# A training step of one transformer block: the backward loop's first four units of exponentials made in the stage ahead of it

## The chip, the cores and the metric

The kernel runs on one core of one Trainium2 chip. The core has five engines with a queue of instructions each: TensorE (PE), VectorE (DVE), ScalarE (ACT), GpSimd (POOL) and SyncE (SP, which here only issues DMAs). Each queue is worked off in order; engines wait for one another through semaphores. The metric is the device time of one execution in microseconds. Before the change it is 2457.15 us, the median of three runs (2454.79 to 2458.89).

## The reference

One block (2048 tokens, width 512, 32 heads of 16, an MLP of 1792 with squared ReLU, modulation from a condition vector c) is run forward, and its vector-Jacobian product is taken for all inputs and weights. Cut to what matters:

```python
h = layernorm(x) * (1 + ca) + sa
qkv = h @ wqkv                                   # 32 heads of 16
p = softmax(q @ k^T / 4)
x = x + ga * ((p @ v) @ wo)
h = layernorm(x) * (1 + cb) + sb
x = x + gb * (relu(h @ w1 + b1) ** 2 @ w2 + b2)
# outputs: x, and the gradients of A_x, wqkv, wo, w1, b1, w2, b2, c, w_mod for a given grad_out
```

## The kernel before, in words

The kernel has four parts that matter here.

*The forward attention loop.* For each of 4 chunks of 512 queries, 8 groups of 4 heads and 16 tiles of 128 keys it makes one unit: scores on PE, exponentials on ACT into a tile ET (128 x 4 x 512, bf16, four buffers), and the product with the values on PE. The MLP, forward and backward, of the chunks already done is woven in between, unit by unit.

*The last stage* (`last_chunk`, line 1265). When the forward loop is over, the MLP of the last chunk of 512 tokens stands alone, from about 1000 to 1101 us. Its order is written out by hand. `dh` (line 1417) makes the gradient at the MLP's input with w1T, a turned copy of w1 that is loaded in seven pieces. `mlp` (line 1469) makes the MLP's output, one token tile of 128 at a time, with 14 matmuls into one PSUM tile; its hooks name work that is put behind the matmul of that number. `grad` (line 1464) makes dO, the gradient of the attention's output, of one token tile. Weight gradients are "chains" (`add_chain`, line 227): four matmuls into a PSUM tile `pc` (three buffers), which DVE adds to a partial sum fetched from DRAM (line 238), and a DMA that stores the result. The four last chains, for out_3, put their results into `iqs` (two), `dpad` and `dwlast`, which SP stores. `later` puts off a DMA by a number of ticks, so the order of SP's queue is that of the ticks. SP's and ACT's DMAs share eight semaphores in turn: a DMA also waits until the one that last used its semaphore has landed. In this stage SP loads the tiles of the first head group, the token-major K (`KS_tok`) and dO of all tokens (`dOs_tok`, lines 1507 to 1509: three quarters from DRAM, the last, line 1518, from SBUF), turns the last chunk's dO by transposing DMAs and stores it.

*The backward attention loop* (line 1784 on). 8 head groups x 4 chunks of keys x 16 tiles of queries = 512 units, in 128 blocks of 4. A unit needs: scores s (4 matmuls, line 1634, in the PSUM banks A, B and C), exponentials e (4 of 128 x 512 on ACT, line 1640, into a tile E_u of four buffers), D (twice: 2 matmuls for dP into psD_u, line 1654, then DVE multiplies it with E_u into dS_u, line 1656), q (k products from dS_u, line 1715, then v products from E_u and dOs_tok, line 1724), a transpose of dS_u by SP's DMA or by PE (t, T), and for each block the dQ products (d, Q). The order within a block is a string of such tokens, one for even and one for odd blocks. D and q run behind the scores: at the start of block b the next D is number 8b - 1 and the next q number 8b - 4, where a number below zero does nothing. f is a keep-warm matmul (`keep_warm`, line 1680) that reads KS_tok and dOs_tok and adds nothing that counts. All queues of the loop, PE's, ACT's, DVE's, SP's and POOL's, follow the order of these strings. POOL clears the tiles of head group 1 at the front of the loop (`head_fill`, line 1785).

*The end*: the gradient at the block's input and of wqkv.

SBUF is given out in pools from two sides. A tile that is put where others lay waits for the last reader and writer of each of them.

## Time and profile before

One execution was profiled: 2456.11 us, with a span of 2454.3 us in the profile and a mean granted clock of 0.989. The median of the three timed runs is 2457.15 us.

| stretch (us) | PE busy | DVE busy | ACT busy | POOL busy | clock |
|---|---|---|---|---|---|
| 1060 to 1080, last stage | 20.00 | 16.84 | 6.36 | 0.00 | 1.00 |
| 1080 to 1100, last stage | 17.88 | 13.73 | 2.10 | 0.00 | 1.00 |
| 1100 to 1120, front of the loop | 17.71 | 14.17 | 13.90 | 8.85 | 0.74 |
| 1120 to 1140 | 19.43 | 18.54 | 18.72 | 0.00 | 1.00 |
| 1160 to 1180 | 19.39 | 19.22 | 19.87 | 1.99 | 1.00 |

Times within the profile are in us from the start of the span. A line of a timeline has the start, the duration, the engine (a q behind its name is its queue, with waits and DMA issues), the line of the kernel, the operation, what it writes <- what it reads, a count where equal instructions are merged, and in brackets how long the engine had stood idle and what ended that. The granted clock is that of TensorE as a share of its full speed.

### The profile page before, as it was taken

The numbers are of one execution on the slowest core, as the hardware profiler recorded it, in microseconds if no ns is written. First come the engines' busy times: TensorE is split into PE (matmuls) and PEld (weight loads), VectorE is DVE, ScalarE is ACT, GpSimd is POOL, SyncE is SP. The second block draws the span as 40 slices with busy tenths as digits, with TensorE's granted clock in tenths as the row PEclk, the third lists the DMA queues.
The fourth block names the chain that finished last, engine by engine and source line by source line (L and its number), as shares of the span: only waits on it lengthen the run. The fifth ranks groups of instructions, "written<-read, shape, count | busy, mean of one in ns | idle before, by whom it ended". The sixth has DMA issues, their size and how long they took to land.

```text
span 2454.3 us, 49932 instructions
## 1 busy us (share of the span) xinstructions
PE 2309.1 (94%) x18994; PEld 775.8 (32%) x18994; DVE 1843.5 (75%) x2390; ACT 2297.7 (94%) x3560; POOL 494.3 (20%) x664
## 2 busy tenths in 40 slices
PE   8899899989998999899999999999999999999999
PEld 3232233223322332442333233323233322323344
DVE  6555464355445554668999999999999989999975
ACT  8999999999998999639999999999999999999964
POOL 3111222332544353300111101101011010110100
PEclk9999999999998999999999999999999989999999
DMA  4578554266647874989999999999999999999995
GB/s 149 135 167 195 177 147 99 85 169 135 96 93 152 153 139 90 237 242 186 209 199 210 205 209 205 203 207 208 204 208 200 204 199 198 208 199 219 200 260 181
DMA packets 1192303, 440.58 MB, mean 180 GB/s; under 512 B 1068283, under 2 KB 1161913, under 8 KB 1191550
## 3 DMA queue, kind: packets, MB, share of 16 engines
q1 hardware_dynamic: 1155214, 392.23, 81.3%
q0 software_dynamic: 19872, 27.09, 7.1%
q10 hardware_dynamic: 16976, 18.07, 2.7%
q8 instruction: 149, 2.44, 0.4%
q14 instruction: 92, 0.75, 0.1%
HBM read 98.83 MB, written 72.63 MB: 70 GB/s over the span
## 4 chain that ended last, share of the span: by engine, by line
ACT 39%; PE 36%; issue 10%; DVE 7%; DMA 5%; POOL 1%; DVEq 0%; SPq 0%; ACTq 0%; POOLq 0%
ACT E_u L1640 24%; ACT ET L580 13%; PE dqacc L1742 5%; PE psST L578 3%; PE psS_A L1634 3%; DMA dsT<-dS_u 3%; PE accVK L1715 2%; PE psS_B L1634 2%; PE psS_C L1634 2%; PE pm L234 2%; PE oacc L594 2%; PE pm L502 2%; PE pdh L1935 2%; PE pm L412 2%; PE pwq L1968 2%
## 5 line engine op out<-in xcount | busy, mean ns | idle before, releaser
L1656 DVE TENSOR_TENSOR dS_u<-psD_u,E_u 128x1024 bf16<-128x1024 f32 x1024 | 1185.4, 1218 | 59.9 <-PE psD_u L1654 19.6
L580 ACT ACTIVATE ET<-psST 128x1024 bf16<-128x1024 f32 x1024 | 941.6, 1268 | 12.6 <-PE psST L578 12.1
L1640 ACT ACTIVATE E_u<-psS_A 128x512 bf16<-128x512 f32 x768 | 496.8, 647 | 8.3 <-PE psS_C L1634 5.9
L1640 ACT ACTIVATE E_u<-psS_B 128x512 bf16<-128x512 f32 x768 | 490.3, 638 | 6.1 <-PE psD_u L1654 1.9
L1654 PE MATMUL psD_u<-iv,ido 32*128 32x512 bf16 x2048 | 408.6, 386 | 0.9 <-DVE dS_u L1656 0.9
L578 PE MATMUL psST<-qt_sb,kt_sb 32*128 32x512 bf16 x2048 | 312.5, 386 | 38.5 <-ACT ET L580 34.8
L1640 ACT ACTIVATE E_u<-psS_C 128x512 bf16<-128x512 f32 x512 | 329.8, 644 | 2.4 <-PE psS_B L1634 0.9
L1634 PE MATMUL psS_A<-ik,iq 32*128 32x512 bf16 x768 | 292.5, 381 | 14.1 <-ACT E_u L1640 1.7
L1634 PE MATMUL psS_B<-ik,iq 32*128 32x512 bf16 x768 | 293.6, 382 | 8.4 <-ACT E_u L1640 1.0
L1763 POOL TENSOR_TENSOR dQacc<-dQacc,dqtmp 128x512 f32<-128x512 f32 x64 | 81.2, 1268 | 838.3 <-ACT dqtmp L1758 838.3
L1634 PEld LDWEIGHTS <-iq 32*128 32x128 bf16 x2048 | 130.4, 91 | 325.3 <-issue 310.4
L1715 PE MATMUL accVK<-dS_u,qz 128*32 128x512 bf16 x2048 | 212.6, 389 | 0.2 <-DVE dS_u L1656 0.2
L594 PE MATMUL oacc<-ET,vaug 128*32 128x512 bf16 x2048 | 207.2, 395 | 3.9 <-DVE ostage L598 3.9
L1724 PE MATMUL accVK<-E_u,dOs_tok 128*16 128x512 bf16 x2048 | 202.5, 384 | 0.0
L1634 PE MATMUL psS_C<-ik,iq 32*128 32x512 bf16 x512 | 194.1, 379 | 4.0
L578 PEld LDWEIGHTS <-kt_sb 32*128 32x128 bf16 x2048 | 84.9, 91 | 316.8 <-issue 298.3
L1742 PE MATMUL dqacc<-dsT,KS_tok 128*32 128x512 bf16 x2048 | 146.7, 384 | 14.8 <-ACT E_u L1640 1.1
L252 DVE COPY part<-pm 128x512 f32<-128x512 f32 (+2 forms) x106 | 65.2, 615 | 120.9 <-PE pm L234 115.2
L1654 PEld LDWEIGHTS <-ido 32*128 32x128 bf16 x2048 | 105.4, 91 | 93.2 <-issue 81.2
L1827 ACT ACTIVATE dsT<-ptT 128x1024 bf16<-128x1024 bf16 x126 | 132.8, 1054 | 1.4 <-PE ptT L1688 1.3
L1715 PEld LDWEIGHTS <-qz 128*32 128x32 bf16 x2048 | 58.3, 94 | 177.1 <-issue 162.2
L1763 POOL TENSOR_TENSOR dQst<-dQacc,dqtmp 128x512 bf16<-128x512 f32 x31 | 39.3, 1267 | 265.1 <-ACT dqtmp L1758 265.1
(423 smaller groups left out, 2672.7 us busy)
## 6 DMA issues: line engine op xcount, KB each, us to landing
p_st<-part POOLq DMA_DIRECT2D x36, 256.0 KB, 4.8
kt_sb<-qkT_st POOLq DMA_DIRECT2D x124, 64.0 KB, 3.3
wA<-in_B_w_dram SPq DMA_DIRECT2D x28, 256.0 KB
wB<-w1T_st SPq DMA_DIRECT2D x21, 256.0 KB
wA<-w2T_st SPq DMA_DIRECT2D x21, 256.0 KB
wB<-in_B_w_dram SPq DMA_DIRECT2D x21, 256.0 KB
p_st<-part POOLq DMA_DIRECT2D x28, 192.0 KB, 4.7
p_st<-part SPq DMA_DIRECT2D x18, 256.0 KB
```

The lines of the kernel that those rows point to most:

```text
L578: PE.matmul(ps[:, hi, :], kt_sb[r:r + 32, kt * P:(kt + 1) * P], qt_sb[r:r + 32, :], start=True, stop=True, tile_position=(r, 0))
L580: ACT.activation(ET[:, 2 * pair:2 * pair + 2, :], ps[:], AF.Exp, scale=SCALE)
L594: PE.matmul(oacc[32 * hq:32 * hq + 32, :], lhsT, ET[:, hq, :], start=(kt == 0), stop=(kt == TT - 1), tile_position=(0, 32 * hq), skip_grou ...
L1634: PE.matmul(psS[:], st["q"][r:r + 32, qt * P:(qt + 1) * P], st["k"][r:r + 32, kc * 512:kc * 512 + 512], start=True, stop=True, tile_positi ...
L1640: ACT.activation(bst[u][0][:, hq, :], sst.pop((u, hq))[:], AF.Exp, scale=SCALE)
L1654: PE.matmul(psD[:, hi, :], st["do"][r:r + 32, qt * P:(qt + 1) * P], st["v"][r:r + 32, kc * 512:kc * 512 + 512], start=True, stop=True, til ...
L1656: DVE.tensor_tensor(dS_u[:, 2 * pair:2 * pair + 2, :], psD[:], E_u[:, 2 * pair:2 * pair + 2, :], ALU.mult)
L1715: PE.matmul(cur["vk"][32 * hq:32 * hq + 32, :], hst[hg]["qz"][:, qt, hq, :], bst[u][1][:, hq, :], start=(qt == 0), stop=False, tile_positi ...
L1724: PE.matmul(acc[32 * hq:32 * hq + DH, :], dOs_tok[:, qt, (hg * 4 + hq) * DH:(hg * 4 + hq + 1) * DH], E_u[:, hq, :], start=False, stop=(qt ...
L1742: PE.matmul(acc[32 * hq:32 * hq + 32, :], KS_tok[:, kc * 4 + kt, h * DH:h * DH + 32], tT[:, :, hq * 4 + kt, :], start=(kt == 0), stop=(kt ...
L1763: POOL.tensor_tensor(dst2, dst, tmp[:], ALU.add)
L1827: ACT.activation(dst, pt[:], AF.Identity)
```

## The change

The exponentials of units 0 to 3, which block 0 of the backward loop made, are now made in the last stage, each unit behind a hook of `mlp` or between two chains. Their tiles come from one pool of four buffers, opened ahead of both loops, that also serves ET, E_u, and w1T in four tiles of up to four pieces' width. dOs_tok no longer has a place during the stage: the last chunk's dO goes to DRAM (`dOs_st`), and all four quarters are loaded by POOL's queue at the front of the loop, into a tile laid out once the stage's pool `dwr` (dpad, xlast, dwlast) is released. Block 0 gets its own string of tokens, without scores and exponentials, with pairs of filler matmuls (i) at its front and keep-warm matmuls among its D and q.

```diff
+    epool = tc.alloc_tile_pool(name="phE", bufs=4, reuse_waits="tile")
+    def exp_tile(name):
+        return epool.tile([P, 4, 512], BF, name=name, tag="E")
...
-            ET = ework.tile([P, 4, 512], BF, name="ET", tag="ET")
+            ET = exp_tile("ET")
...
-                    PE.matmul(pdh[:], dzT[:, fc, ti * P:(ti + 1) * P], w1T[:, fc, :],
+                    PE.matmul(pdh[:], dzT[:, fc, ti * P:(ti + 1) * P], w1T[fc // 4][:, fc % 4, :],
...
+            def first_exps(u, tags):
+                keep["E", u] = E = exp_tile("E_u")
+                acc = [pools["mm"].tile([P, 512], F32, name="psSe", tag=t, bufs=3 if t == "pc" else 4) for t in tags]
+                for hq in range(4):
+                    r = 32 * hq
+                    PE.matmul(acc[hq][:], hsets[0]["q"][r:r + 32, u * P:(u + 1) * P], hsets[0]["k"][r:r + 32, 0:512],
+                              start=True, stop=True, tile_position=(r, 0))
+                for hq in range(4):
+                    ACT.activation(E[:, hq, :], acc[hq][:], AF.Exp, scale=SCALE)
...
-            keep["dOs"] = dpool.tile([P, TT, D], BF, name="dOs_tok", tag="dt")
-            for i in range(QC - 1):
-                later(2 + 2 * i, sp, keep["dOs"][:, 4 * i:4 * i + 4, :], dOs_st[:, 4 * i:4 * i + 4, :])
             mlp(0, {5: lambda: finish_dx(3), 7: lambda: turn_da(2), 11: lambda: grad(1)})
             sp(dx1_st[:, ts, :], dx1_c)
-            mlp(1, {3: lambda: turn_da(3), 7: lambda: grad(2)})
-            mlp(2, {3: lambda: grad(3)})
+            mlp(1, {3: lambda: turn_da(3), 7: lambda: grad(2), 12: lambda: first_exps(0, ("pc", "pc", "pc", "pm"))})
+            mlp(2, {3: lambda: grad(3), 9: lambda: first_exps(1, ("pc", "pc", "pm", "pm"))})
...
-            later(1, sp, keep["dOs"][:, ts, :], dOs_c[:])
+            later(1, sp, dOs_st[:, ts, :], dOs_c[:])
             store_grad(c, 1, dOT, dlt, 1)
-            mlp(3, {5: head_do})
+            mlp(3, {5: head_do, 10: lambda: first_exps(2, ("pc", "pc", "pm", "pm"))})
...
-            fill(3)
+            fill(2)
+            first_exps(3, ("pm",) * 4)
+            fill(1)
             flush_sums(True)
...
-                dpool = tc.alloc_tile_pool(name="dpool", bufs=1, reuse_waits="tile", side="right")
                 dwr = tc.alloc_tile_pool(name="dwr", bufs=1, reuse_waits="tile", side="right")
-                w1T = dpool.tile([P, FC, D], BF, name="w1T_1", tag="dt")
+                w1T = [exp_tile("w1T_1") for _ in range(4)]
...
-                    sp(w1T[:, 2 * s:2 * s + 2, :], w1T_st[:, 2 * s:2 * s + 2, :])
+                    sp(w1T[s // 2][:, 2 * (s % 2):2 * (s % 2) + 2, :], w1T_st[:, 2 * s:2 * s + 2, :])
...
         dwr.release()
-    KS_tok, dOs_tok = keep["KS"], keep["dOs"]
+    dpool = tc.alloc_tile_pool(name="dpool", bufs=1, reuse_waits="tile", side="right")
+    KS_tok, dOs_tok = keep["KS"], dpool.tile([P, TT, D], BF, name="dOs_tok", tag="dt")
...
-                bst[u] = [ework.tile([P, 4, 512], BF, name="E_u", tag="E_u"), None]
+                bst[u] = [exp_tile("E_u"), None]
...
+        order_0 = (
+            "i D i D i D q q q q q f f D q D f f D q f f D f q D f f ").split(), ""
         load_head(0)
+        for u in range(4):
+            bst[u] = [keep["E", u], None]
...
+            for i in range(QC):
+                POOL.dma_start(out=dOs_tok[:, 4 * i:4 * i + 4, :], in_=dOs_st[:, 4 * i:4 * i + 4, :])
             head_fill(1)
...
-                toks, bank = order_t if on_pe(b - 1) else order_n
+                toks, bank = order_0 if b == 0 else order_t if on_pe(b - 1) else order_n
...
-                        if b < 2 and i % 2 == 1:
-                            if nq > 0:
-                                keep_warm()
-                            elif nq < 0:
-                                PE.matmul(idle[:], ones_bf[:], identb.unsqueeze(1).to_broadcast([P, 4, P]), start=True, stop=True)
+                        if b == 1 and i % 2 == 1:
+                            keep_warm()
+                    elif c == "i":
+                        for _ in range(2):
+                            PE.matmul(idle[:], ones_bf[:], identb.unsqueeze(1).to_broadcast([P, 4, P]), start=True, stop=True)
```

More of the change, by code (lines that the diff above doesn't have):

```diff
@@ L1834 @@
         dq_last = hst[HG - 1]["dq"]
+    epool.release()
     with ExitStack() as ph:
```

## The prediction

> **What bounds the kernel now.** I read the page first, then the busy time by stretches of 20 us, the timeline of each engine between 1080 and 1130 us (the end of the dense stage and the front of the backward loop), the issues of DMAs, and the granted clock by stretches of 1 us.

> The page: busy share and instructions of each engine, and the chain that ended last.

> ```profile
> PE 2309.1 (94%) x18994; PEld 775.8 (32%) x18994; DVE 1843.5 (75%) x2390; ACT 2297.7 (94%) x3560; POOL 494.3 (20%) x664
> ACT 39%; PE 36%; issue 10%; DVE 7%; DMA 5%; POOL 1%; DVEq 0%; SPq 0%; ACTq 0%; POOLq 0%
> ```

> PE and ACT are both full on average, so an exponential moved out of the loop is worth something only where it is not replaced by another limit. The change touches about 50 us. By stretches (busy us of PE, PEld, DVE, ACT, POOL; granted clock; DMA share; GB/s):

> ```profile
> 1080.00:1100.00 20.00, 17.88 (x87) 7.48 (x85) 13.73 (x27) 2.10 (x8) 0.00 (x0) 1.00 0.90 241
> 1100.00:1120.00 20.00, 17.71 (x99) 4.00 (x98) 14.17 (x14) 13.90 (x26) 8.85 (x5) 0.74 0.92 216
> 1140.00:1160.00 20.00, 19.45 (x196) 6.02 (x188) 19.35 (x18) 19.96 (x40) 0.00 (x0) 1.00 1.19 221
> ```

> ACT has 18 us of 20 free before the loop, DVE loses about 5 us in the loop's first 20, and from 1140 PE, DVE and ACT are all at 97% or more. Timeline at the border:

> ```profile
> 1086.13 0.41 DVE L238 TENSOR_TENSOR dwbuf<-pc,dwbuf 128x256 bf16<-128x256 f32 x1
> 1090.06 0.38 PE L267 MATMUL rsums<-gfprod,ones_bf 128*1 128x512 bf16 x1 [1.50 <-DVE gfprod L1479]
> 1100.27 0.68 DVE L238 TENSOR_TENSOR dwlast<-pc,part 128x512 bf16<-128x512 f32 x1
> 1101.00 0.37 PE L1634 MATMUL psS_A<-ik,iq 32*128 32x512 bf16 x1 [0.86 <-DVE dwlast L238]
> 1110.10 0.60 PE L1681 MATMUL accVK<-dOs_tok,KS_tok 128*16 128x512 bf16 x1
> 1112.99 0.60 PE L1634 MATMUL psS_C<-ik,iq 32*128 32x512 bf16 x1
> 1124.08 0.39 PE L1634 MATMUL psS_A<-ik,iq 32*128 32x512 bf16 x1
> ```

> The stage ends with DVE's dwlast at 1100.95. PE starts the loop's block 0 at 1101.00, block 1 at 1112.99, block 2 at 1124.08: 12.0 and 11.1 us, where a later block takes (2344.3 - 1124.5)/126 = 9.68 us (start of block 2's first exponential to the end of the last, 126 blocks). So 3.7 us is all that the ramp of these two blocks can give back. PE first reads dOs_tok at 1110.10. SP's queue in the same time:

> ```profile
> 1088.56 0.32 SPq L179 DMA_DIRECT2D dx_st<-dx_c  x1
> 1093.72 5.62 SPq L179 DMA_TRANSPOSE dOT<-dOs_c  x4
> 1107.84 0.40 SPq L179 DMA_DIRECT2D out_dram<-dwlast  x1
> ```

> and issues by POOL (KB each, median us to landing), with the clock by 1 us:

> ```profile
> p_st<-part POOLq DMA_DIRECT2D x36, 256.0 KB, 4.8
> kt_sb<-qkT_st POOLq DMA_DIRECT2D x124, 64.0 KB, 3.3
> ```
> ```profile
> 1104.00:1105.00 1.00, 0.71 (x3) 0.28 (x3) 1.00 (x2) 0.57 (x2) 1.00 (x2) 0.87 0.99 352
> 1105.00:1106.00 1.00, 0.93 (x2) 0.10 (x1) 0.14 (x1) 0.82 (x3) 1.00 (x1) 0.50 0.50 143
> 1114.00:1115.00 1.00, 1.00 (x9) 0.10 (x1) 0.97 (x1) 0.72 (x2) 0.00 (x0) 0.51 1.29 215
> ```

> The clock was 0.50 from 1104.9 to 1115.0, though PE was busy for nearly all of it.

> **The change, part by part.**

> *Four batches of first exponentials in the stage.* 16 score matmuls and 16 exponentials of 128x512 move forward; the list of instructions of the changed program shows them there, and from block 1 on PE's and ACT's lists are as before. ACT has the room (2.10 us busy of 20). PE has not (17.88 of 20). The first batch stands behind the 13th matmul of the second tile's product, which PE reaches at 1083.5, and takes the three pc buffers at once. DVE empties two of them at 1083.88 and 1086.13 (row above, 0.41 us), and the third score waits for an exponential, which stands in ACT's queue behind delta's copies and two stores that now issue until 1087.4. So PE goes on at about 1088.5: 5.0 us late. Of this 1.5 us comes back: PE's wait for gfprod (1090.06 row) ends with a DVE operation that itself waits for a p_st fetch until 1088.98, and that stays. A wait of 0.63 us for dpad at 1093.49 is covered as well. The other three batches find free buffers: 4 scores each, about 0.4 us by PE's rows. Sum 5.0 - 1.5 - 0.6 + 3 x 0.4 = +4.1 us on the stage. Bounds: +1.6 (four batches at 0.4, no wait), +6.2 (nothing comes back). dwlast is then evicted at 1105.1.

> *The load of dOs_tok moves behind the stage.* Before, SP loads three quarters at 1085.7 to 1092 and the last comes from SBUF at 1100.05. Now SP loses three issues of some 0.4 us, and the stage 1.5 MB, at 241 GB/s 6.5 us of transfer. That takes nothing off PE there; it lets SP begin the dOT transposes at about 1091 instead of 1093.72 (dx_st need not share the queues) and reach the out_3 stores by about 1105. The new tile lies over dpad, xlast and dwlast, so POOL's first load waits for the stores of all three. Hence a chain: dwlast at 1105.1, its store issued at 1105.6, landed 2.2 us later, then 512 KB through POOL's queue. The store is not shown landing. Bounds: 1.5 us (rows_st issued 1108.29, its waiter on POOL starts 1109.75, 2 KB) and 5.1 us (a 96 KB store on the chain of waits, 1042.17, when the DMAs were full); 2.2 is near the lower because the big stores are out by then. The load: 3.3 us (64 KB, above) to 5.2 us (the 512 KB dx_st store, 1088.56 to the transposes that waited for it, 1093.72); 5.0 because 256 KB by POOL already has 4.8, though that one accumulates. It lands at 1105.6 + 2.2 + 5.0 = 1112.8.

> [...]

> *Who waits.* On PE, in order: idle fillers, scores D0 and D1, the k products of unit 0, then a keep-warm filler that reads dOs_tok. DVE can do two dS operations (until about 1108); D2 stands behind the filler. PE stands from about 1108.4 to 1112.8. From that filler to block 1 PE has 17 steps (9 fillers, 5 D, 3 q). At half clock the starts lie 0.55 us apart (1108.12, 1108.65, 1109.20), at full clock 0.32 (1116.21, 1116.53, 1116.84): 9.3 or 5.4 us; DVE alone needs some 5.1. After 4 us of standing I take the half clock for most of it: 8.0. Block 1 starts at 1120.8. It takes between 9.7 (a steady block) and 11.1 us (before, 2 us of it at half clock): 10.6. Block 2 starts at 1131.4, against 1124.1: +7.3 us.

> *The rest.* POOL's five memsets of 1.80 us (head 1's tiles and qz, 1101.06 to 1111.55) stand behind the four load issues; their readers start about 17 units (41 us) later, which hides them; without that cover up to 9 us. The other three quarters of dOs_tok, some 2.4 us each at 216 GB/s, land by about 1120 and are read from block 1 on: 0, at worst 2 us. w1T in four tiles of the exponentials' pool: the same seven loads behind the same forward loop, 0. Eight filler matmuls more, counted above. The last stage has the same instructions with tiles elsewhere: 0, within 1 us either way.

> Sum: 2456.1 (the profiled execution, span 2454.3) + 7.3 = 2463.4. The median of the runs shown is 1.0 above that execution: **2464.4 us**.

> **The rivals.** 0.2%, or 4.9 us, is about what a measurement of this kernel can tell from no change.

> *The loads land in time, not slower.* Its point is one: dOs_tok's first quarter must land before PE asks, at about 1108. If the first batch costs PE only its 0.4 us (stage +1.6), dwlast is out at 1102.6, and with 1.5 and 3.3 us the quarter lands at 1107.9; block 1 at 1113.3, a steady block 1, block 2 at 1123.0: 1.1 us less, 2456.0. For it: ACT is empty, and DMA traffic leaves the stage. Against: the three pc buffers, and SP's queue, which reached that store only at 1107.84. To fall under 2452.2 the stage would also have to be shorter, by the DMA waits that I left as they are (4.5 us at 1079.55 and 4.3 at 1084.56 stand in the chain).

> *The wait stays, but PE keeps or regains the full clock.* 5.4 us instead of 8.0, block 1 in 9.9 instead of 10.6: +4.0, 2461.2. For it: at 1012 to 1016 the clock was half for only some 3 us. Against: 10 us at the loop's front, with the same mix of small products. [...]

> *A longer wait.* The store takes 5.1 us and the load 5.2 with clock and block 1 at their bad ends: 1105.6 + 5.1 + 5.2 + 9.3 + 11.1 = 1136.3, +12.2, 2469.3.

> **How the numbers follow.** The forecast 0.60, the longer wait 0.10: both slower by over 0.2%. The full clock 0.16, within 0.2%. Loads in time 0.14, of which 0.08 faster and 0.06 within. So faster 0.08, same 0.22, slower 0.70. The range goes from the loads in time, 2456, to the longer wait, 2470; some 0.1 lies below and 0.05 above.

> **What would show it.** Exponentials' tiles written between 1084 and 1104 with ACT still mostly idle; PE waiting for DVE's dwbuf in the middle of the second product; POOL's first dOs_tok issue only after the store of dwlast; PE standing over 3 us for a DMA in front of the keep-warm filler, DVE idle with it; block 2 some 7 us later. Wrong if that filler starts without a wait, if the stage's end moves by under 2 us, or if PE goes at full clock from the wait on.

## The result, and the profile after

The changed kernel takes 2465.81 us (median of 22 executions, 2458.87 to 2473.56); the kernel before, measured beside it, 2457.02 us (median of 22, 2453.65 to 2467.78). The ratio is 1.0037, with a 95% interval of 1.0024 to 1.0049: slower, by 0.24% to 0.49%. The profiled execution took 2464.85 us, with a span of 2463.0 us. That is 8.7 us more than the profiled one of before.

The page of the changed kernel, busy share of each engine and the chain that ended last:

```profile
PE 2312.3 (94%) x19002; PEld 775.0 (31%) x19002; DVE 1843.9 (75%) x2390; ACT 2297.8 (93%) x3560; POOL 496.6 (20%) x668
ACT 38%; PE 37%; issue 10%; DVE 8%; DMA 4%; POOL 1%; SPq 0%; ACTq 0%; DVEq 0%; POOLq 0%
```

The sums are those of before to within 4 us: the same work, ordered otherwise. What changed lies in a few stretches (columns: busy us of PE, PEld, DVE, ACT, POOL; granted clock; DMA share; GB/s):

```profile
1080.00:1100.00 20.00, 17.39 (x74) 6.84 (x73) 11.22 (x21) 6.29 (x18) 0.00 (x0) 0.83 0.68 178
1100.00:1120.00 20.00, 14.96 (x73) 4.21 (x72) 10.27 (x15) 4.73 (x9) 9.01 (x8) 0.81 0.63 214
1140.00:1160.00 20.00, 19.27 (x195) 6.16 (x187) 19.35 (x17) 19.87 (x39) 0.00 (x0) 1.00 1.08 170
```

ACT takes exponentials between 1080 and 1100, as intended. But the clock there fell from 1.00 to a mean of 0.83, and in the next stretch PE and DVE are emptier than before, 14.96 and 10.27 us instead of 17.71 and 14.17. From 1140 on the two kernels are alike. PE's timeline (start, duration, line, what it writes; in brackets how long it stood idle and what ended that) shows three stands:

```profile
1085.17 0.39 PE L1508 MATMUL psSe<-ik,iq 32*128 32x512 bf16 x1
1086.77 0.37 PE L1508 MATMUL psSe<-ik,iq 32*128 32x512 bf16 x1 [1.22 <-DVE dwbuf L243]
1088.54 0.61 PE L1508 MATMUL psSe<-ik,iq 32*128 32x512 bf16 x2 [1.39 <-ACT E_u L1511]
1090.15 1.89 PE L1477 MATMUL pm<-w,sT 128*128 128x512 bf16 x4
...
1115.51 1.01 PE L1695 MATMUL accVK<-dOs_tok,KS_tok 128*16 128x512 bf16 x2 [3.81 <-DMA dOs_tok<-dOs_st]
1123.30 0.38 PE L1648 MATMUL psS_C<-ik,iq 32*128 32x512 bf16 x1
1133.55 0.39 PE L1648 MATMUL psS_A<-ik,iq 32*128 32x512 bf16 x1
```

The first batch of scores waits 1.22 us for a PSUM buffer that DVE empties and 1.39 us for an exponential. Behind it four matmuls take 1.89 us, where four of the same shape took 1.03 us at 1083.15. At the loop's front PE stands 3.81 us for dOs_tok. Block 1 begins at 1123.30 and block 2 at 1133.55; before, block 2 began at 1124.08. The chain of waits between the stage and the loop, in order of time (start, duration, what):

```profile
1107.76 0.62 DVE dwlast L243
1108.51 1.80 DMA out_dram<-dwlast
1110.46 0.53 issue
1110.99 4.47 DMA dOs_tok<-dOs_st
```

Result, store, landing, load, in a row: 7.7 us in which the loop gets nothing new. SP's queue came to that store no sooner, either: it issued store after store ahead of it, with 0.1 us between these lines.

```profile
1104.78 1.71 SPq L184 DMA_DIRECT2D d_st<-dltT  x4
1106.59 0.37 SPq L184 DMA_DIRECT2D out_dram<-xlast  x1
1107.05 0.86 SPq L184 DMA_DIRECT2D out_dram<-iqs  x2
1108.01 0.41 SPq L184 DMA_DIRECT2D out_dram<-dpad  x1
```

The last of these ends at 1108.42; dwlast is ready at 1108.38. The clock by stretches of 1 us:

```profile
1088.00:1089.00 1.00, 0.46 (x2) 0.10 (x1) 0.00 (x0) 0.97 (x2) 0.00 (x0) 0.69 1.03 357
1095.00:1096.00 1.00, 1.00 (x8) 0.50 (x6) 0.97 (x2) 0.25 (x2) 0.00 (x0) 0.90 0.64 129
...
1112.00:1113.00 1.00, 0.00 (x0) 0.00 (x0) 0.00 (x0) 0.00 (x0) 1.00 (x3) 0.63 0.52 131
1122.00:1123.00 1.00, 1.00 (x9) 0.20 (x4) 0.94 (x2) 0.00 (x0) 0.02 (x1) 0.75 1.18 218
```

Between these lines it is 0.50. A stretch with 0.69 has 0.62 us at half clock, so the clock fell at 1088.38; in the same way it rose at 1095.20, fell again at 1112.26 and rose at 1122.50. Each of the two long waits is followed by several us at half clock, though PE is busy again, from 1089 and from 1115.5 on. The second fall came 0.6 us into the long stand; two shorter waits for DVE, 0.49 and 0.73 us, lay just ahead of it (1109.7 to 1111.3).

Where the 8.7 us come from, by one marker: the second chain of four 128x256 products in `mlp(1)` (1082.77 before, 1084.41 after) lies ahead of the first early exponential. It is 1.64 us late already. Up to there only tile places and SP's loads differ, and in the other executions below this marker lies anywhere between 1082 and 1090, so I count that part to the execution and not to the change. From the marker to the start of the stage's last chain it is 16.34 us before and 22.19 after: +5.85. Two more executions of that stage (the kernel before with fillers behind the stage, below) took 16.92 and 17.66 us, so this difference is good to about 1.3 us. From the marker to block 2 it is 41.31 and 49.14: +7.83. Behind block 2, 0.8 us comes back; the execution of before had half clock there for 13.64 us (2005.86 to 2019.50), that of the changed kernel for 6.82 (1515.04 to 1521.86), so I do not count that part to the change either.

### The profile page after: what moved, and what is told of

Its sections match the earlier page's. It is cut to its first block, busy times and chain, and to the rows that moved or that the text cites. A ratio compares the mean times of both kernels' runs of the same rounds, so it can differ in the third digit from the quotient of the medians.

```text
span 2463.0 us, 49951 instructions
## 1 busy us (share of the span) xinstructions
PE 2312.3 (94%) x19002; PEld 775.0 (31%) x19002; DVE 1843.9 (75%) x2390; ACT 2297.8 (93%) x3560; POOL 496.6 (20%) x668
## 4 chain that ended last, share of the span: by engine, by line
ACT 38%; PE 37%; issue 10%; DVE 8%; DMA 4%; POOL 1%; SPq 0%; ACTq 0%; DVEq 0%; POOLq 0%
ACT E_u L1654 23%; ACT ET L585 12%; PE dqacc L1756 4%; PE psST L583 3%; PE psS_A L1648 3%; PE accVK L1729 2%; PE psS_B L1648 2%; PE pm L239 2%; PE psS_C L1648 2%; PE oacc L599 2%; DMA dsT<-dS_u 2%; PE pm L507 2%; PE pdh L1956 2%; PE pm L417 2%; PE pwq L1989 2%
## 5 line engine op out<-in xcount | busy, mean ns | idle before, releaser
L1756 PE MATMUL dqacc<-dsT,KS_tok 128*32 128x512 bf16 x2048 | 146.7, 384 | 15.8 <-DMA iq<-qkT_st 2.2
## 6 DMA issues: line engine op xcount, KB each, us to landing
p_st<-part POOLq DMA_DIRECT2D x36, 256.0 KB, 4.8
wA<-in_B_w_dram SPq DMA_DIRECT2D x28, 256.0 KB
wB<-w1T_st SPq DMA_DIRECT2D x21, 256.0 KB
wA<-w2T_st SPq DMA_DIRECT2D x21, 256.0 KB
wB<-in_B_w_dram SPq DMA_DIRECT2D x21, 256.0 KB
p_st<-part SPq DMA_DIRECT2D x18, 256.0 KB
```

The lines of the kernel that those rows point to most:

```text
L1756: PE.matmul(acc[32 * hq:32 * hq + 32, :], KS_tok[:, kc * 4 + kt, h * DH:h * DH + 32], tT[:, :, hq * 4 + kt, :], start=(kt == 0), stop=(kt ...
```

## The experiments

Theory at the start: the loss is two waits (the PSUM buffers of the first batch; the load of dO behind the stage's last store) and the half clock that each leaves behind. Rivals: the batches cost by their place or number alone; the load is late for its own sake; the half clock costs nothing. Single executions lie up to 17 us from their kernel's median, so the places are read from the profiles and the verdict from the medians of 6 to 12 executions. All kernels compute the same; the fillers add zero to an accumulator or write a tile that nobody reads. Two distances are used throughout: from the first batch's first score to the loop's first filler ("stage"), and from that filler to block 1's first score ("front").

| kernel | median us | ratio to before (95%) | stage us | front us |
|---|---|---|---|---|
| the change | 2465.81 | 1.0037 (1.0024 to 1.0049) | 22.31 | 15.82 |
| results in tiles of their own | 2462.56 | 1.0012 (0.9997 to 1.0027) | 22.26 | 11.62 |
| batches later in the stage | 2466.55 | 1.0035 (1.0015 to 1.0055) | moved | 16.15 |
| fillers in both waits | 2460.19 | 1.0003 (0.9986 to 1.0021) | 20.48 | 13.67 |
| loads behind the memsets | 2473.85 | 1.0059 (1.0036 to 1.0081) | 22.10 | 21.85 |
| fillers in the stage alone | 2463.91 | 1.0028 (1.0011 to 1.0045) | 20.30 | 16.61 |
| fillers at the front alone | 2464.04 | 1.0027 (1.0011 to 1.0043) | 22.61 | 13.79 |
| own tiles and fillers | 2458.69 | 1.0004 (0.9990 to 1.0018) | 19.72 | 10.43 |
| before, with fillers | 2456.53 | 0.9988 (0.9971 to 1.0006) | | |
| the same again | 2459.85 | 1.0001 (0.9988 to 1.0014) | | |
| late load alone | 2460.03 | 1.0021 (1.0001 to 1.0041) | | |

The medians of before beside them were 2459.21 (first four), 2457.71 (next four) and 2458.42 us (last two). Where two kernels were measured beside different ones of these, the text compares their distances to the kernel before.

### The late results in tiles of their own

dpad, dwlast and xlast no longer lie where dOs_tok is put, so POOL's load waits for none of their stores.

```diff
-            xlast = dwr.tile([P, D], BF, name="xlast")
...
+            late_c = cb.tile([P, 4, D], BF, name="late_c", tag="xn2_c")
+            xlast = late_c[:, 0, :]
...
-            L_late.extend((qs[:, 0:D], qs[:, D:2 * D], dpad.rearrange("p t h d -> p (t h d)"),
-                            dwr.tile([P, D], BF, name="dwlast", tag="proda")[:]))
+            L_late.extend((qs[:, 0:D], qs[:, D:2 * D], late_c[:, 1, :], late_c[:, 2, :]))
```

> The changed kernel, but xlast and the results of the last two out_3 chains go into a dead tile of the stage (that of xn2_c) instead of dwr, so that dOs_tok lies over nothing that is stored late. Theory (the wait for dOs_tok's first quarter costs standing time and the half clock after it): POOL's first load issues at about 1100 to 1102 instead of 1111, PE does not stand in front of the first keep-warm filler (3.8 us before), the clock stays full, and block 1 starts some 9.5 us after PE's first filler of the loop instead of 15.8: about 6 us less than the changed kernel, some 2460. Rival (the loop would take the lost time back, or the wait only moves to the dS operations): PE's wait goes, but block 2 starts within 2 us of where it does now, and the time stays at 2464 to 2467.

Measured: 2462.56 us. POOL's first loads go at 1099.61 instead of 1110.99, and the wait for the DMA is gone. The timelines of POOL and PE of this kernel, and two stretches of 1 us:

```profile
1099.61 1.70 POOL L1804 DMA_DIRECT2D dOs_tok<-dOs_st  x3 [55.78 <-DVE x_c L1488]
```
```profile
1108.92 0.39 PE L1729 MATMUL accVK<-dS_u,qz 128*32 128x512 bf16 x2 [0.55 <-DVE dS_u L1670]
1110.05 0.49 PE L1729 MATMUL accVK<-dS_u,qz 128*32 128x512 bf16 x2 [0.74 <-DVE dS_u L1670]
1110.06 0.91 PE L1695 MATMUL accVK<-dOs_tok,KS_tok 128*16 128x512 bf16 x2
1117.79 0.39 PE L1648 MATMUL psS_C<-ik,iq 32*128 32x512 bf16 x1
```
```profile
1109.00:1110.00 1.00, 0.32 (x2) 0.02 (x3) 1.00 (x1) 0.00 (x0) 0.00 (x0) 1.00 1.06 416
1111.00:1112.00 1.00, 1.00 (x8) 0.13 (x6) 0.38 (x1) 0.00 (x0) 0.00 (x0) 0.50 0.95 315
```

The front is 4.2 us shorter. That the load waits for the stores is shown. The front stayed longer than the theory wanted, since the clock fell even without the long stand: two waits for DVE of 0.55 and 0.74 us, with PE busy for 0.77 of the 2 us from 1108 to 1110, came ahead of it, and it stayed at 0.50 until 1117.

### The batches later in the stage

The first batch goes behind the last matmul of the third tile, the next two into the fourth, with two pc buffers each.

```diff
-            mlp(1, {3: lambda: turn_da(3), 7: lambda: grad(2), 12: lambda: first_exps(0, ("pc", "pc", "pc", "pm"))})
-            mlp(2, {3: lambda: grad(3), 9: lambda: first_exps(1, ("pc", "pc", "pm", "pm"))})
+            mlp(1, {3: lambda: turn_da(3), 7: lambda: grad(2)})
+            mlp(2, {3: lambda: grad(3), 13: lambda: first_exps(0, ("pc", "pc", "pm", "pm"))})
...
-            mlp(3, {5: head_do, 10: lambda: first_exps(2, ("pc", "pc", "pm", "pm"))})
+            mlp(3, {5: head_do, 9: lambda: first_exps(1, ("pc", "pc", "pm", "pm")), 13: lambda: first_exps(2, ("pc", "pc", "pm", "pm"))})
```

> The changed kernel, but the four batches of first exponentials stand later: behind the third tile's last matmul, behind matmuls 10 and 14 of the fourth tile, and the last as before. Theory (the first batch holds PE back because it takes the three pc buffers before DVE has emptied them, and the standing brings the half clock at 1089 to 1095): the batches find buffers free within about 1 us, the clock stays full, and the stage ends 3 to 4.5 us earlier: about 2462. Rival (the stage is longer because PE has 16 more products to do and ACT's exponentials delay its other work, wherever they stand): the stage ends within 1 us of where it does now, 2465 to 2466.

Measured: 2466.55 us, level with the change. PE still waits, for the same kind of DVE work, and DVE itself has waited for a p_st fetch (its timeline, second fence):

```profile
1096.01 0.61 PE L1508 MATMUL psSe<-ik,iq 32*128 32x512 bf16 x3 [2.01 <-DVE dwbuf L243]
```
```profile
1091.70 0.42 DVE L243 TENSOR_TENSOR dwbuf<-pc,dwbuf 128x256 bf16<-128x256 f32 x1 [3.14 <-DMA dwbuf<-p_st]
```

From the marker (1085.58 here) to the last chain (1106.28) the stage takes 20.70 us, 1.5 less than with the change and 4.4 more than before: between the theory (3 to 4.5 us earlier) and the rival (within 1 us). The clock did not stay full either; it fell behind the wait, from 1095.50 to 1098.90. So the wait moves with the batch, and this place bought little of the time back.

### Fillers in both waits

Five matmuls that add zero ahead of the second and the third score of the first batch, and twelve ahead of the keep-warm filler that waits for dOs_tok. No wait is taken away; PE is only kept busy in them.

```diff
                 for hq in range(4):
                     r = 32 * hq
+                    for _ in range(5 if u == 0 and hq in (1, 2) else 0):
+                        PE.matmul(pools["rs"][0:DH, :], zeros[:], identb.unsqueeze(1).to_broadcast([P, 4, P]), start=False, stop=False,
+                                  tile_position=(0, 0), skip_group_check=True)
...
-            "i D i D i D q q q q q f f D q D f f D q f f D f q D f f ").split(), ""
+            "i D i D i D q q q q q w f f D q D f f D q f f D f q D f f ").split(), ""
...
+                    elif c == "w":
+                        for _ in range(12):
+                            PE.matmul(cur["vk"][0:DH, :], zeros[:], identb.unsqueeze(1).to_broadcast([P, 4, P]), start=False, stop=False,
+                                      tile_position=(0, 0), skip_group_check=True)
```

> The changed kernel with filler matmuls that add zeros where PE stands: 5 each ahead of the second and third score of the first batch, and 12 ahead of the first keep-warm filler of block 0. Theory (of what the waits cost, a part is the half clock behind them): the granted clock stays 1.00 from 1085 to 1130, the waits themselves stay as long, the products behind the first batch take 1.03 us per four instead of 1.89, and block 1 starts 5.5 to 6 us after dOs_tok's landing instead of 7.8: 1.5 us less in the stage and 2 us less in block 0, about 2462.5. Rival (block 0 goes at DVE's rate, not at PE's): block 1 still starts 7 to 8 us after the landing, and only the stage's 1.5 us go: 2464 or more.

Measured: 2460.19 us, level with before. PE's and DVE's timelines:

```profile
1111.68 0.59 PE L1698 MATMUL accVK<-dOs_tok,KS_tok 128*16 128x512 bf16 x2 [1.41 <-DMA dOs_tok<-dOs_st]
1117.35 0.39 PE L1651 MATMUL psS_C<-ik,iq 32*128 32x512 bf16 x1
```
```profile
1112.71 8.06 DVE L1673 TENSOR_TENSOR dS_u<-psD_u,E_u 128x1024 bf16<-128x1024 f32 x7 [5.25 <-PE psD_u L1671]
```

POOL issues the load 3.50 us behind the loop's first filler (3.51 in the changed kernel) and DVE still loses 5.25 us, so the load is as late as it was. But the clock stays at 1.00 through both places, the stage is 1.8 us shorter, and from the landing to block 1 it takes 5.7 us instead of 7.8. The half clock is a cost of its own, in both places. The two distances together are 4.0 us shorter; the median, 1.0 us over the kernel before instead of 8.8, fell by more than these places explain, though the intervals allow for both.

### The loads behind the memsets

The load is made later still: POOL does its five memsets first.

```diff
-            for i in range(QC):
-                POOL.dma_start(out=dOs_tok[:, 4 * i:4 * i + 4, :], in_=dOs_st[:, 4 * i:4 * i + 4, :])
             head_fill(1)
             POOL.memset(qz[1][:], 0.0)
+            for i in range(QC):
+                POOL.dma_start(out=dOs_tok[:, 4 * i:4 * i + 4, :], in_=dOs_st[:, 4 * i:4 * i + 4, :])
```

> The changed kernel, but POOL's five memsets (about 1.8 us each) stand ahead of the four loads of dOs_tok instead of behind them. Theory (the landing of the first quarter sets when block 0 goes on): the loads issue some 6 to 9 us later (the first memsets need not wait for the late stores, so a part of the 9 us lies beside that wait), PE stands that much longer, and the time grows by as much: 2472 to 2475. Rival (the landing is not what sets the end, or the loop takes it back): under 2 us more.

Measured: 2473.85 us, 14.6 us over the kernel before where the change has 8.8. POOL and PE:

```profile
1116.45 2.23 POOL L1806 DMA_DIRECT2D dOs_tok<-dOs_st  x4
```
```profile
1121.21 1.01 PE L1695 MATMUL accVK<-dOs_tok,KS_tok 128*16 128x512 bf16 x2 [9.56 <-DMA dOs_tok<-dOs_st]
```

The issue is 5.46 us later than in the changed kernel, block 1 5.98 us, and the time 5.9 us longer. What the load is late by reaches the end in full, as far as six executions can tell (0.36% to 0.81% over the kernel before).

### Each place alone

The edits are those of the two fillers above, one at a time.

> The changed kernel with five zero-adding matmuls ahead of the second and the third score of the first batch, and nothing at the loop's front. Theory (two separate costs of the half clock): the stage, from the first score to the loop's first filler, goes back from 22.3 us to the 20.5 us that it had with fillers in both places, the front of the loop, from that filler to block 1's first score, stays at 15.8 us, and the time falls by about 2 us, to 2463.5 us (bounds 2462 to 2465). Rival (one cost: whatever the loop's front does follows from the stage's disturbed clock): the front shrinks too, to 13.7 us, and the time falls by 4 us, to 2461.5 us.

> The changed kernel with twelve zero-adding matmuls ahead of block 0's first keep-warm filler, and nothing in the stage. Theory (two separate costs): the stage stays at 22.3 us, the front of the loop goes from 15.8 to 13.7 us, the PE stands for the first quarter as before, and the time falls by about 2 us, to 2463.5 us (bounds 2462 to 2465). Rival (the half clock at the front costs nothing, since the loop's later parts set the time): the front shrinks and the time stays at 2465 to 2467 us.

Measured: 2463.91 and 2464.04 us, each about 2 us under the change, as the theory of two separate costs expected. The distances moved apart in the same way: 20.30 and 16.61 us, 22.61 and 13.79 us. The intervals of these two are wider than the difference, so the distances carry the reading, not the medians. From the marker to the last chain the first of them takes 20.19 us: with the full clock the change lengthens the stage by 3.85 us against the profile of before, and by 3.3 and 2.5 us against the two other executions of that stage.

The profile of the first one holds a surprise (clock by 1 us; PE idle in the first line, waiting for the load):

```profile
1113.00:1114.00 1.00, 0.00 (x0) 0.00 (x0) 0.00 (x0) 0.00 (x0) 1.00 (x2) 0.50 0.90 287
1130.00:1131.00 1.00, 1.00 (x8) 0.13 (x4) 0.17 (x1) 0.53 (x2) 0.00 (x0) 0.50 1.24 220
1146.00:1147.00 1.00, 1.00 (x11) 0.38 (x9) 0.00 (x0) 0.45 (x1) 0.00 (x0) 0.50 0.00 0
1147.00:1148.00 1.00, 1.00 (x9) 0.19 (x3) 0.80 (x1) 1.00 (x3) 0.00 (x0) 0.94 0.00 0
```

Here the half clock lasted 34.1 us, from 1113.0 to 1147.12, with PE busy from 1114.65 on. This execution took 2471.38 us, 7.5 over its kernel's median.

### No wait and no half clock

Own tiles for the late results, the fillers in the stage, and nine fillers around the first k products at the front. The first two edits are those above; w stands for four matmuls here.

```diff
+                for _ in range(3 if u == 0 and hq == 1 else 0):
+                    PE.matmul(cur["vk"][0:DH, :], zeros[:], identb.unsqueeze(1).to_broadcast([P, 4, P]), start=False, stop=False,
+                              tile_position=(0, 0), skip_group_check=True)
...
-            "i D i D i D q q q q q f f D q D f f D q f f D f q D f f ").split(), ""
+            "i D i D i D i q q q q q w f f D q D f f D q f f D f q D f f ").split(), ""
```

> The changed kernel with the two late results (and the last rows of the stage's first output) in tiles of their own, so that the first load of dO waits for no store, and with fillers in both stands of the PE: five ahead of the second and third score, two ahead of the first dK quad, three inside it and four behind it. Theory (wait and half clock together are the whole loss): stage 20.5 us, front 9.5 to 10.5 us, no wait for the quarter, block 1 some 7 to 8 us earlier against the first score than in the changed kernel; time 2458 us (2456 to 2460), that is level with the kernel before, and nothing gained over it. Rival (the exponentials made ahead are worth more, once the losses are gone): below 2455 us, faster than the kernel before. Second rival (the fillers themselves take time on a full PE): 2460 to 2463 us.

Measured: 2458.69 us, level with before: the first theory, neither rival. From the first score to block 1 it takes 30.15 us against 38.13 with the change. So the loss is accounted for. The question that is left is where the gain is, with 16 exponentials less in block 0. The stretch of block 0 in this kernel, from the loop's first filler to block 1:

```profile
1110.83:1121.26 10.43, 9.68 (x55) 2.65 (x54) 7.89 (x9) 0.01 (x1) 1.18 (x1) 1.00 0.77 260
```

ACT does nothing and PE is busy for 9.68 of 10.43 us, but 24 of PE's 55 matmuls there are fillers: 8 that write `idle`, 9 keep-warm products and 7 that add zero (2.24, 2.70 and 1.84 us busy). They are not free. DVE, which has seven dS operations of some 1.15 us to do with or without exponentials, stands 1.96 us for a D that PE reaches only behind six of them:

```profile
1116.62 8.07 DVE L1673 TENSOR_TENSOR dS_u<-psD_u,E_u 128x1024 bf16<-128x1024 f32 x7 [1.96 <-PE psD_u L1671]
```

So a full PE is not shown to be what this block needs; a string with fewer fillers was not run. The next kernel has the same place with the exponentials in it.

### The kernel before, with fillers

```diff
+            for _ in range(3):
+                PE.matmul(idle[:], ones_bf[:], identb.unsqueeze(1).to_broadcast([P, 4, P]), start=True, stop=True)
             for b in range(NU // 4 + 3):
...
                             elif nq < 0:
-                                PE.matmul(idle[:], ones_bf[:], identb.unsqueeze(1).to_broadcast([P, 4, P]), start=True, stop=True)
+                                for _ in range(2):
+                                    PE.matmul(idle[:], ones_bf[:], identb.unsqueeze(1).to_broadcast([P, 4, P]), start=True, stop=True)
```

> The kernel before with three more fillers ahead of the loop's first score and two instead of one behind every second exponential of block 0. It has the half clock at its own loop front too, for 10.1 us from 1104.9. Theory: if the fillers hold the full clock, the first two blocks lose 2 to 4 us and the time falls to 2453 to 2455 us, so that the fair comparison for fillers is this kernel; block 2 begins 2 to 4 us earlier against the stage's last chain (24.97 us in the kernel before). Rival: the ACT sets the pace of the first two blocks whatever the clock, and the time stays at 2456 to 2458 us.

> The kernel before with the same fillers at its loop front as in the run of that kernel above, measured a second time for a narrower interval. Theory (the half clock at the loop's front costs the kernel before 2.5 us, as its second block begins 22.4 instead of 25.0 us behind the stage's last chain): 2455 to 2456 us, ratio 0.999 or below. Rival: level with the kernel before, ratio 1.000.

Measured: 2456.53 and 2459.85 us, ratios 0.9988 and 1.0001. The clock stays at 1.00 at the loop's front, and block 2 begins 22.44 and 22.43 us behind the start of the stage's last chain instead of 24.97. The 2.5 us are there in both profiles, but the two medians together neither show them nor rule them out. Block 0 of the first one, from its first score to block 1's, and a piece of its chain of waits:

```profile
1102.80:1112.83 10.03, 9.19 (x58) 2.33 (x58) 6.97 (x7) 8.39 (x16) 8.63 (x5) 1.00 0.66 209
```
```profile
1103.22 2.55 ACT E_u L1640 x5
```

The two blocks do not start alike, so I count both from the start of the stage's last chain. Block 1 begins 11.93 us behind it with 16 exponentials on ACT and 11.30 us without them, block 2 22.44 and 21.83 us. The first exponentials do stand in the chain of waits, but with these fillers on PE taking all 16 out shortens the front by only 0.6 us. The stage pays more than that: from the marker to the last chain it takes 19.72 us with the early batches, at the full clock, and 16.34, 16.92 and 17.66 us in the three executions of the kernel before. No version here is shown to be faster than the kernel before.

### The late load alone

The early exponentials are undone; the pools and the loads behind the stage stay.

```diff
-            mlp(1, {3: lambda: turn_da(3), 7: lambda: grad(2), 12: lambda: first_exps(0, ("pc", "pc", "pc", "pm"))})
+            mlp(1, {3: lambda: turn_da(3), 7: lambda: grad(2)})
...
-                toks, bank = order_0 if b == 0 else order_t if on_pe(b - 1) else order_n
+                toks, bank = order_t if on_pe(b - 1) else order_n
...
```

> The changed kernel without its early exponentials: the four batches are gone from the stage, and block 0 makes its exponentials itself in the order of the kernel before. What stays of the change is the one pool, the weight in four tiles and the four quarters of dO loaded behind the stage's last stores. Theory (the loads are late only because block 0 lost its cover): the quarter lands some 8.9 us behind the start of the stage's last chain, as in the changed kernel, the first filler that reads it comes 11 us behind that chain, as in the kernel before, so nothing waits, and the time is that of the kernel before, 2457.5 us (2456 to 2459). Rival (the late load costs by itself): the first filler of block 0 waits some us for the load, and the time is above 2461 us.

Measured: 2460.03 us, by its median between the two. The ratio, 1.0021 (1.0001 to 1.0041), lies above that of the medians, as four of the twelve executions took 2467 us or more; these four have a mean clock of 0.982 to 0.986, the others 0.987 to 0.993. The theory's step on the landing fell, and the rival's wait is there. DVE's, SP's and PE's timelines:

```profile
1099.50 0.68 DVE L243 TENSOR_TENSOR dwlast<-pc,part 128x512 bf16<-128x512 f32 x1
```
```profile
1090.83 5.16 SPq L184 DMA_TRANSPOSE dOT<-dOs_c  x4
1099.17 0.51 SPq L184 DMA_DIRECT2D dOT_st<-dOT  x1
1100.47 1.72 SPq L184 DMA_DIRECT2D d_st<-dltT  x4
1104.21 0.40 SPq L184 DMA_DIRECT2D out_dram<-dwlast  x1
```
```profile
1111.51 0.59 PE L1693 MATMUL accVK<-dOs_tok,KS_tok 128*16 128x512 bf16 x1 [2.08 <-DMA dOs_tok<-dOs_st]
```

dwlast is ready at 1100.18, but its store stands in SP's queue behind the transposes and the stores of dO until 1104.21. So the load lands 13.2 us behind the start of the last chain (1098.34) and not 8.9, and PE waits 2.08 us. A stage that ends early does not make the load early: SP's queue is the second limit, here about 4 us behind the first. The stage itself takes 15.91 us from the marker to the last chain, no more than before, so the new tile places alone do not lengthen it. The profiled execution was at half clock from 1103.46 to 1137.58.

## Why the prediction was right, and which terms were off

The forecast was 2464.4 us, slower; measured 2465.81. The mechanism holds: ACT had room and PE had not, PE waited for pc buffers, the load waited for the store of dwlast, PE stood in front of the keep-warm filler and DVE with it. Term by term, from the profile of the changed kernel:

- *The stage, +4.1 us predicted, +5.85 measured.* The first batch's stand was 3.9 us from the first score to the next matmul of the tile (1085.17 to 1089.08), not 5.0. What the step lacked is the clock: it fell at 1088.38, in the stand, and was 0.50 until 1095.20; four matmuls behind the stand took 1.89 us instead of 1.03. With fillers in the stand the stage is 3.85 us longer than in the profile of before, near the 4.1; the missing term is 2.0 us. The prediction applied the half clock at the loop's front, for a stand of 4.4 us, and left it out here, where it had 5.0.
- *Store and load, 7.7 us from the result to the landing predicted, 7.1 measured*: 0.14 to the issue instead of 0.5, 2.48 to POOL's issue instead of 2.2, 4.52 instead of 5.0 for 512 KB. SP came to the first out_3 store at 1107.05 and not by about 1105; that this cost nothing is luck, as dwlast was ready only when SP's queue got to it.
- *PE's stand, 4.4 predicted, 3.81 measured. The rest of block 0, 8.0 predicted, 7.8 measured* at 0.50; with the clock held it is 5.7, where the prediction's lower bound was 5.4. *Block 1: 10.6 and 10.25. Block 2: +7.3 and +7.83*, with the marker's 1.64 us taken off.
- *The terms at zero* (memsets, the other quarters, the weight in four tiles, the end): up to block 2 nothing waits for them in the profile.
- *The median, predicted 1.0 us above the profiled execution*, was 0.96 above it; with executions from 2458.87 to 2473.56 us, that is luck. The 1.4 us by which the forecast is short are some 0.5 up to block 2 and the 1.64 ahead of the marker, less the 0.8 behind block 2; no step has the last two. That the sum up to block 2 is off by only 0.5 is luck in part: the steps' errors (+1.75, -0.6, -0.2, -0.35) partly cancel.

The rivals: *loads in time* needed a stage of +1.6 and a store that goes at once. The late load alone shows that it was further off than it looked, because SP issues that store 4 us after the result even when the stage is short. *Full clock kept* is what the fillers made: 1.0 us over the kernel before, where that rival had 4.0; the interval (up to 1.0021) holds both. Where the stand at the loop's front had no fillers, the half clock went on behind it: in the changed kernel it lasted 7.0 us more from the load's landing (1115.5 to 1122.5) with PE busy, and with fillers in the stage alone some 32 us (1114.65 to 1147.12). *The longer wait* did not come unless the loads were put later by hand.

The bound of the gain, 3.7 us from the ramp of the first two blocks, held, but little of it belonged to the exponentials. With the wait for the load and the half clock gone the changed kernel reaches block 2 21.83 us behind the start of the stage's last chain, 3.14 sooner than the kernel before. Fillers alone give that kernel 2.53 of them, with its exponentials in place. The 0.6 that are left for the early exponentials are less than the 2.1 to 3.4 us that making them costs the stage. Whether a block 0 with fewer fillers would give back more stays open.

## What to carry to other kernels

Work that is moved to an engine that looks idle is not free: before moving it to fill a hole, see what its old place gains without it (0.6 us here), and count what it takes on the other engines at the new one (PSUM buffers, for which PE waited 1.22 us on DVE and 1.39 us on an exponential; the tile space that pushes a load behind a store, 7.1 us from the result to the landing). A stand of PE cost its length here and then about 2 us more by half clock; a few products that add zero in the stand saved that second part (the stage 1.8 us shorter, block 1 5.7 us behind the landing instead of 7.8). Where a load has been put behind a store, look for the store in its queue: with the late load alone it went when SP's queue got to it, 4.0 us after the result was ready.

## What was not expected of the hardware

*The clock fell without a whole step of standing.* With the results in tiles of their own, waits of 0.55 and 0.74 us with little work between them lay just ahead of the fall at 1110.22. In the 3.41 us ahead of the fall PE was busy for some 2.12 us there (3.41 less the two waits), for 1.62 ahead of the fall at 1112.26 in the changed kernel, and for 2.60 ahead of the one at the front of the kernel before.

*The scatter between executions follows the clock.* Over the 86 executions of the kernel before that were measured beside the experiments, the time falls by 2.0 us for each 0.001 of mean granted clock (correlation -0.81; 2.4, 1.8 and 1.5 us in the three sets by themselves); 0.001 of the span is 4.9 us at half clock. Why one stretch lasts two steps and another ten stays open; no view of these profiles tells it.
